# First block of a fused attention and two-layer kernel: attention rounds that overlap, low halves made on VectorE instead of GpSimd, and w_in stored in 4 KB rows

## The chip, the cores and the metric

One core of a Trainium2 chip runs the whole program. The metric is the device time of one execution in microseconds (us). A profiled execution has a span of its own, from the first to the last instruction that the trace shows, and a time beside it.

## The reference

The input is q, k and v of 4 batches, 8 heads, 576 positions and 64 dimensions, so 2304 tokens of width 512. Three layers follow each other.

```
scores = q @ k.T / 8, kept where 0 <= i - j < 64     # sliding window
x  = softmax(scores) @ v                              # 2304 x 512
h  = x @ w_in                                         # 512 -> 2048
x2 = softplus(h) @ w_out                              # max(h,0) + log1p(exp(-|h|)), 2048 -> 512
e  = argmax(x2 @ w_gate + bias[modality]),  p = softmax at e
out = p * (relu(x2 @ w1[e]) @ w2[e])                  # 8 experts, 512 -> 1024 -> 512
```

w_in and w_out come as 64-bit floats. Products are wanted to float32 accuracy.

## The kernel before

TensorE multiplies in a rounded float32 (F32R), so each operand is split: a high half (the value cast to F32R) and a low half (the value minus its high half, made by the helper `diff`, L88). A product is the sum of three matmuls: high by high, high by low, low by high.

The tokens are cut into 6 blocks of 384 (`b`), the 2048 hidden columns into 16 slices of 128 (`f`). A block's attention is 6 chunks of 64 tokens (`c`, so chunks 0 to 5 belong to block 0). One chunk goes through `a_scores` (scores and mask on TensorE, row maximum on VectorE, exponentials on ScalarE), `a_norm` (VectorE: reciprocal of the sum; the multiplication on VectorE for block 0 and on GpSimd for the others), `a_probs` (transposes on TensorE, copy on ScalarE) and `a_av` (times v on TensorE; `xh` by ScalarE, `xl` by VectorE). Tiles: `pss` scores, `s` probabilities, `pp` transposes, `pav` the product with v.

`mm1(b, f)` makes the hidden slice `ph` from 12 matmuls, which read the block's whole `xh` and `xl`, so it can't start before the last chunk's halves are there. It then makes softplus and its halves `gh` and `gl`. `mm2(b, f)` adds the slice to the three accumulators `px` with 9 matmuls, two slices later (LAG = 2). One such step is called a round here.

While block 0 runs, the weights are made as well: `w_load(f)` fetches 1 MB of slice f (half of it w_in, half w_out) into `raw`, and `w_decode(f)` turns the 64-bit floats into float32 by integer steps: ScalarE takes the absolute value (L222), VectorE clamps, shifts, and merges (L225 to L228), ScalarE casts the high half (L229), GpSimd makes the low half (L88 with tile `W`). The tile `wt` between L222 and L227 exists once. Slices 0 to 2 are decoded in two halves (w_in, then w_out). All weights stay on the chip, so blocks 1 to 5 have no decode.

Names for lines: L245 VectorE sets the sign bit, so that -|h| goes into the exponential; L246 and L247 are the exponential and logarithm on ScalarE, L248 adds max(h, 0) on VectorE, L251 casts `gh`. A scheduler orders each engine's instructions when the kernel is built; on the chip each engine then runs its list in order. `HOLD` makes it wait: the decodes of slices 1 and 2 come after the probabilities of chunks 4 and 5.

Of the kernel before, what the change touches and what calls it, by code (L numbers as in the profile page):

```python
# [19 lines left out]
P = 128  # L20
# [14 lines left out]
def attention_moe_moe_kernel(ctx, tc, q, k, v, w_in, w_out, modality, w_gate, mod_bias, w1, w2, out):  # L35
# [3 lines left out]
    HD = 64  # L39
    H = D // HD  # L40
    N = B * S
    F = w_in.shape[1]
    E, _, F2 = w1.shape
    KD = D // P
    NF = F // P
# [41 lines left out]
    def diff(eng, out_, a, hi):  # L87
        eng.tensor_tensor(out_, a, hi.bitcast(F32), ALU.subtract)  # L88

    at = {}  # L90
    marks = {}
    xblk = {}


# [22 lines left out]
    def a_scores(c, tags=None, s=None):  # L117
        w = at[c]
        win, n, qT, kT = w["win"], w["n"], w["q"], w["k"]
        if tags is None:  # L120
            both = ps.tile([P, 2, 4, P], F32, name="pss", tag="pS")
            parts = [both[:, :, 0:2, 0:n]]
            bank = [both[:, z, 0:2, 0:n] for z in range(2)]
        else:
            bank = [ps.tile([P, 2, P], F32, name=f"pss{z}", tag=tags[0], bufs=tags[1])[:, :, 0:n] for z in range(2)]
            parts = [x[:, None] for x in bank]
        for i in range(2):
            heads = [(2 * i + e, z) for e in range(2) for z in range(2)]
            outs = [bank[z][half(j, z) * C:(half(j, z) + 1) * C, i, :] for j, z in heads]
            for (j, z), o in zip(heads, outs):  # L130
                r = slice(z * C, (z + 1) * C)
                nc.tensor.matmul(o, qT[r, j, :], kT[r, :, j, :], start=True, stop=c >= BUSY)
            if c < BUSY:
                for (j, z), o in zip(heads, outs):
                    r = slice(z * C, (z + 1) * C)
                    nc.tensor.matmul(o, identb[r, r], mask[r, win], start=False, stop=True)
        s = sb.tile([P, 2, 2, P], F32, name="s") if s is None else s
        if c >= BUSY:
            nc.vector.tensor_tensor(s[:, :, :, 0:n], parts[0], mask[:, None, None, win].to_broadcast((P, 2, 2, n)), ALU.add)
            parts = [s[:, :, :, 0:n]]  # L140
            bank = [s[:, z, :, 0:n] for z in range(2)]
        mx = sb.tile([P, 2, 2], F32, name="mx")
        for i, x in enumerate(parts):
            nc.vector.tensor_reduce(out=mx[:, i:i + x.shape[1]], in_=x, axis=AX.X, op=ALU.max)
        nc.vector.tensor_scalar(mx, mx, -SCALE, None, ALU.mult)
        sm = sb.tile([P, NPR], F32, name="sm")
        for z in range(2):
            for i in range(2):
                marks['e', c] = nc.scalar.activation(s[:, z, i, 0:n], bank[z][:, i, :], AF.Exp, bias=mx[:, z, i:i + 1], scale=SCALE, accum_out=sm[:, 2 * z + i:2 * z + i + 1])
        w.update(s=s.rearrange("p z i k -> p (z i) k"), sm=sm)  # L150

    def a_norm(c):
        s, sm, n = at[c]["s"], at[c].pop("sm"), at[c]["n"]
        nc.vector.tensor_scalar(sm, sm, 1e-9, None, ALU.add)
        nc.vector.reciprocal(sm, sm)  # L155
        marks['n', c] = (nc.vector if c < CPB else nc.gpsimd).tensor_tensor(s[:, :, 0:n], s[:, :, 0:n], sm[:, :, None].to_broadcast((P, NPR, n)), ALU.mult)  # L156

    def a_probs(c, tag="pA", bufs=1, pT=None):
        s, n = at[c].pop("s"), at[c]["n"]
        pp = ps.tile([P, NPR, P], F32, name="pp", tag=tag, bufs=bufs)  # L160
        for j in range(NPR):
            nc.tensor.transpose(pp[0:n, j, :], s[:, j, 0:n], ident)
        pT = sb.tile([P, NPR, P], F32, name="pT", bufs=1) if pT is None else pT
        marks['p', c] = nc.scalar.copy(pT[0:n], pp[0:n])
        at[c]["pT"] = pT

    def a_av(c, tag="pA"):
        pT, n, vr = at[c].pop("pT"), at[c]["n"], at[c]["vr"]
        if c % CPB == 0:
            xblk[c // CPB] = (sb.tile([P, KD, TB], F32R, name="xh"), sb.tile([P, KD, TB], F32R, name="xl"))  # L170
        xh, xl = xblk[c // CPB]
        col = slice((c % CPB) * C, (c % CPB + 1) * C)
        po = ps.tile([P, NPR, C], F32, name="pav", tag=tag)
        for j in range(NPR):
            for z in range(2):
                r = slice(z * C, (z + 1) * C)
                nc.tensor.matmul(po[r, j, :], vr[0:n, j * P + z * C:j * P + (z + 1) * C], pT[0:n, 2 * z + j // 2, half(j, z) * C:(half(j, z) + 1) * C], start=True, stop=True)
        marks['v', c] = nc.scalar.copy(xh[:, :, col], po)
        diff(nc.vector, xl[:, :, col], po, xh[:, :, col])

    def attn_slots(b):
# [13 lines left out]

    W = {}
    raws = {}
    HOLD = {1: ('p', 4), 2: ('p', 5)}

    def wait_for(later, earlier, reason):  # L200
        tc.add_manual_dep(later.ins, earlier.ins.name, mybir.DependencyInfo(mybir.DependencyClass.Sync, mybir.DependencyReason.DATA), reason=reason)
# [1 line left out]
    def w_load(f, half=None):  # L203
# [1 line left out]
            raws[f] = wp.tile([P, 2, 512, 2], I32, name="raw", tag="W")  # L205
        raw = raws[f]
        if half != 1:
            nc.sync.dma_start(
                raw[:, 0].rearrange("p (k f) w -> p k (f w)", k=KD),
                w_in.bitcast(I32).rearrange("(k p) (f w) -> p k f w", p=P, w=2)[:, :, f * P:(f + 1) * P, :].rearrange("p k f w -> p k (f w)"))  # L210
        if half != 0:
            nc.sync.dma_start(raw[:, 1].rearrange("p f w -> p (f w)"), w_out.bitcast(I32)[f * P:(f + 1) * P, :])

    def w_decode(f):
# [20 lines left out]
    def mm1(b, f):  # L235
# [18 lines left out]

    px = {}
# [619 lines left out]
```

## Time and profile before

| what | us |
|---|---|
| median of 3 runs (lowest, highest) | 803.86 (803.25, 804.68) |
| the profiled execution: time | 805.67 |
| the profiled execution: span | 803.8 |
| mean granted TensorE clock in it | 0.968 |
| busy in the span: TensorE matmul / VectorE / ScalarE / GpSimd | 744.1 / 464.0 / 348.4 / 311.6 |

The time of an execution is about 2 us longer than its span, and the profiled one was some 2 us above the median of the others. The shares are averages over the attention of block 0, the rounds of block 0 with their decodes, five blocks without decodes, and the routed experts behind them.

### The profile page before, as it was taken

The page shows a single profiled execution, that of the slowest core. Times are in us where ns is not written, and L with a number is a line of the kernel's source. Part 1 is how long each engine was busy: PE and PEld are TensorE (multiplying, and loading weights), DVE is VectorE, ACT ScalarE, POOL GpSimd, SP SyncE. Part 2 cuts the span into 40 slices and gives each one's busy share as a digit, 9 for nine tenths or more (in the row PEclk, how much of TensorE's full clock was granted, in tenths as well). Part 3 has the DMA queues.
Part 4 walks back from the last instruction along what each step waited for, and adds up shares of the span by engine and source line. Part 5 has one row for each costly group of instructions (what it writes and reads, how often), then busy time and mean ns, then how long its engine had stood idle before and what let it go on. Part 6 is the DMA issues. An engine that isn't in the chain of part 4 may idle for free. (4 is left out here: it accounts for less than half of the span.)

```text
span 803.8 us, 12803 instructions
## 1 busy us (share of the span) xinstructions
PE 744.1 (93%) x4527; PEld 623.2 (78%) x4527; DVE 464.0 (58%) x1030; ACT 348.4 (43%) x827; POOL 311.6 (39%) x309
## 2 busy tenths in 40 slices
PE   5568878999999999999999999989989999999995
PEld 4457667888878888888878888878868888888884
DVE  4899999397459533964298428863533223223242
ACT  4655556554454554545355543544222122222243
POOL 3247565332423421342233322472273443443301
PEclk9669999999999999999999999999999999999998
DMA  8846531510232111311040103315021111111100
GB/s 316 250 153 206 167 107 46 178 53 21 60 100 66 35 46 44 108 27 48 14 144 1 28 14 112 138 32 231 15 73 37 55 48 36 52 52 45 39 28 17
DMA packets 48411, 65.17 MB, mean 81 GB/s; under 512 B 12797, under 2 KB 33661, under 8 KB 48200
## 3 DMA queue, kind: packets, MB, share of 16 engines
q1 hardware_dynamic: 43800, 54.45, 21.0%
q0 software_dynamic: 4528, 9.74, 3.7%
q8 instruction: 37, 0.61, 0.3%
q14 instruction: 46, 0.38, 0.2%
HBM read 54.37 MB, written 10.06 MB: 80 GB/s over the span
## 5 line engine op out<-in xcount | busy, mean ns | idle before, releaser
L88 POOL TENSOR_TENSOR gl<-a,gh 128x384 fp32r<-128x384 f32 x96 | 112.4, 1172 | 203.7 <-ACT gh L251 104.1
L240 PE MATMUL ph<-xh,W 128*128 128x384 f32 x384 | 136.8, 359 | 15.2 <-DVE a L248 14.9
L241 PE MATMUL ph<-xl,W 128*128 128x384 f32 x384 | 134.5, 350 | 0.8 <-DVE xl L88 0.8
L242 PE MATMUL ph<-xh,W 128*128 128x384 f32 x384 | 133.6, 348 | 0.0
L264 PE MATMUL px<-W,gh 128*128 128x512 f32 x288 | 115.9, 402 | 0.0
L265 PE MATMUL px<-W,gh 128*128 128x512 f32 x288 | 114.0, 396 | 0.0
L266 PE MATMUL px<-W,gl 128*128 128x512 f32 x288 | 105.9, 400 | 1.2 <-POOL gl L88 1.1
L246 ACT ACTIVATE a<-a 128x384 f32<-128x384 f32 x96 | 50.3, 524 | 116.4 <-DVE a L245 116.3
L240 PEld LDWEIGHTS ph<-xh,W 128*128 128x128 f32 x384 | 75.0, 196 | 24.6 <-DVE a L248 18.9
L245 DVE TENSOR_SCALAR a<-ph 128x384 int32<-128x384 int32 x96 | 52.9, 551 | 54.1 <-PE ph L242 52.2
L626 POOL DMA_INDIRECT gx<-x2s,pieces x76 | 73.7, 970 | 23.6 <-issue 13.9
L248 DVE SCALAR_TENSOR_TENSOR a<-ph,a 128x384 f32<-128x384 f32 x96 | 53.0, 552 | 45.5 <-ACT a L247 45.3
L241 PEld LDWEIGHTS ph<-xl,W 128*128 128x128 f32 x384 | 75.0, 195 | 4.7 <-DVE xl L88 1.6
L242 PEld LDWEIGHTS ph<-xh,W 128*128 128x128 f32 x384 | 74.8, 195 | 0.2
L251 ACT CAST gh<-a 128x384 fp32r<-128x384 f32 x96 | 49.1, 512 | 48.9 <-DVE a L248 45.0
L266 PEld LDWEIGHTS px<-W,gl 128*128 128x128 f32 x288 | 53.1, 188 | 14.1 <-POOL gl L88 2.5
L655 PE MATMUL p<-w,x2h 128*128 128x512 f32 x152 | 62.5, 411 | 1.2 <-ACT x2h L641 1.2
L88 POOL TENSOR_TENSOR W<-raw,W 128x1024 fp32r<-128x1024 f32 (+1 forms) x19 | 44.3, 2332 | 48.0 <-ACT W L229 48.0
L156 POOL TENSOR_TENSOR s<-s,sm 128x512 f32<-128x512 f32 (+1 forms) x30 | 34.5, 1150 | 72.6 <-DVE sm L155 51.1
L264 PEld LDWEIGHTS px<-W,gh 128*128 128x128 f32 x288 | 54.1, 188 | 10.9 <-issue 1.7
L693 POOL DMA_INDIRECT out_dram<-o,mg x19 | 19.3, 1017 | 107.8 <-ACT o L692 102.3
L265 PEld LDWEIGHTS px<-W,gh 128*128 128x128 f32 x288 | 54.3, 188 | 8.6
(192 smaller groups left out, 1420.5 us busy)
## 6 DMA issues: line engine op xcount, KB each, us to landing
raw<-in_moe_w_in_dram SPq DMA_DIRECT2D x16, 512.0 KB
raw<-in_moe_w_out_dram SPq DMA_DIRECT2D x16, 512.0 KB
r<-in_moe_w_dram SPq DMA_DIRECT2D x8, 1024.0 KB
qk<-in_k_dram SPq DMA_DIRECT2D x27, 256.0 KB
vr<-in_v_dram SPq DMA_DIRECT2D x27, 256.0 KB
qk<-in_q_dram SPq DMA_DIRECT2D x30, 128.0 KB
x2s<-xr SPq DMA_DIRECT2D x15, 256.0 KB
early<-in_v_dram SPq DMA_DIRECT2D x5, 256.0 KB
```

The source lines that it names most:

```text
L88: eng.tensor_tensor(out_, a, hi.bitcast(F32), ALU.subtract)
L240: nc.tensor.matmul(ph, W[f][:, 0, 0, sl], xh[:, c, :], start=c == 0, stop=False)
L241: nc.tensor.matmul(ph, W[f][:, 0, 0, sl], xl[:, c, :], start=False, stop=False)
L242: nc.tensor.matmul(ph, W[f][:, 0, 1, sl], xh[:, c, :], start=False, stop=c == KD - 1)
L245: nc.vector.tensor_scalar(a.bitcast(I32), ph.bitcast(I32), SIGN, None, ALU.bitwise_or)
L246: nc.scalar.activation(a, a, AF.Exp)
L248: nc.vector.scalar_tensor_tensor(a, ph, 0.0, a, ALU.max, ALU.add)
L264: nc.tensor.matmul(px[b][t], gh[:, sl], W[f][:, 1, 0, :], start=f == 0, stop=False)
L265: nc.tensor.matmul(px[b][t], gh[:, sl], W[f][:, 1, 1, :], start=False, stop=False)
L266: step["mm2"] = nc.tensor.matmul(px[b][t], gl[:, sl], W[f][:, 1, 0, :], start=False, stop=f == NF - 1)
L626: g = nc.gpsimd.indirect_dma_start(out=xr[:, c].rearrange("p c d -> p (c d)"), out_offset=None, in_=x2s[0:rows, :].rearrange("n (r f) -> ( ...
L655: first = nc.tensor.matmul(p, ah(c), bh(c), start=c == 0, stop=False)
```

## The change

Four things change, all in the part of the program that runs until block 0 is done.

1. Attention of block 0: the loop over rounds starts the scores of chunk i before it finishes chunk i-1, puts the product with v one round later (i-3), and the two `HOLD` waits go. The decodes of slices 0 and 1 are written into rounds 1 and 6 instead of 3 and 7. The order of the first loads changes with it.
2. Low halves: `W`'s are made by VectorE in every decode, `gl` by VectorE in block 0 and by GpSimd after it.
3. In block 0 ScalarE takes the absolute value of `ph` and a scale of -1 in the exponential, instead of VectorE's sign step. For block 1's attention (chunks 6 to 11) ScalarE multiplies by the reciprocals, four activations to a chunk, instead of one GpSimd operation.
4. w_in lies in memory by slice, 128 rows of 4 KB to a slice, instead of four runs of 1 KB to a row.

```diff
     def a_norm(c):
...
-        marks['n', c] = (nc.vector if c < CPB else nc.gpsimd).tensor_tensor(s[:, :, 0:n], s[:, :, 0:n], sm[:, :, None].to_broadcast((P, NPR, n)), ALU.mult)
+        if CPB <= c < BUSY:
+            for i in range(NPR):
+                nc.scalar.activation(s[:, i, 0:n], s[:, i, 0:n], AF.Copy, scale=sm[:, i:i + 1])
+        else:
+            (nc.vector if c < CPB else nc.gpsimd).tensor_tensor(s[:, :, 0:n], s[:, :, 0:n], sm[:, :, None].to_broadcast((P, NPR, n)), ALU.mult)
...
-    HOLD = {1: ('p', 4), 2: ('p', 5)}
...
-            nc.sync.dma_start(
-                raw[:, 0].rearrange("p (k f) w -> p k (f w)", k=KD),
-                w_in.bitcast(I32).rearrange("(k p) (f w) -> p k f w", p=P, w=2)[:, :, f * P:(f + 1) * P, :].rearrange("p k f w -> p k (f w)"))
+            nc.sync.dma_start(raw[:, 0].rearrange("p f w -> p (f w)"), w_in.bitcast(I32)[f])
...
-            d_ = nc.scalar.activation(tf, hf, AF.Abs)
-            if f in HOLD:
-                wait_for(d_, marks[HOLD[f]], 'attention first')
+            nc.scalar.activation(tf, hf, AF.Abs)
...
-            diff(nc.gpsimd, w[:, h, 1, :], hf, w[:, h, 0, :])
+            diff(nc.vector, w[:, h, 1, :], hf, w[:, h, 0, :])
...
-        nc.vector.tensor_scalar(a.bitcast(I32), ph.bitcast(I32), SIGN, None, ALU.bitwise_or)
-        nc.scalar.activation(a, a, AF.Exp)
+
+        if b == 0:
+            nc.scalar.activation(a, ph, AF.Abs)
+            nc.scalar.activation(a, a, AF.Exp, scale=-1.0)
+        else:
+            nc.vector.tensor_scalar(a.bitcast(I32), ph.bitcast(I32), SIGN, None, ALU.bitwise_or)
+            nc.scalar.activation(a, a, AF.Exp)
...
-        diff(nc.gpsimd, gl, a, gh)
+        diff(nc.gpsimd if b else nc.vector, gl, a, gh)
...
-    for part, c in [('qk', 0), ('qk', 1), ('v', 0), (0, 0), ('qk', 2), ('v', 1), ('v', 2), ('v', 3), ('v', 4), ('v', 5), (0, 1), (1, 0), (0, 2), (1, 1), (1, 2), ('qk', 6), ('v', 6), (0, 3), (1, 3)]:
+    for part, c in [('qk', 0), (0, 0), ('qk', 1), ('v', 0), (1, 0), ('qk', 2), ('v', 1), ('v', 2), ('v', 3), (0, 1), ('v', 4), ('v', 5), (1, 1), (0, 2), (1, 2), ('qk', 6), ('v', 6), (0, 3), (1, 3)]:
...
-    for i in range(CPB + 2):
+    for i in range(CPB + 3):
+        if i < CPB:
+            a_scores(i, ("px", TPB) if i % 2 else None, sb.tile([P, 2, 2, P], F32, name="s0", tag="xo", bufs=3))
+        if i in [1, 6]:
+            w_decode([1, 6].index(i))
         if 1 <= i <= CPB:
             a_norm(i - 1)
-        if i >= 2:
+        if i >= 3:
+            a_av(i - 3)
+        if 2 <= i < CPB + 2:
             a_probs(i - 2, "ph", 2, work if i % 2 else None)
-        if i >= 2:
-            a_av(i - 2)
-        if i < CPB:
-            a_scores(i, ("px", TPB) if i % 2 else None, sb.tile([P, 2, 2, P], F32, name="s0", tag="xo", bufs=3))
-        if i in [3, 7]:
-            w_decode([3, 7].index(i))
```

The engines' lists move at three places. The first is VectorE's list before, one round in the second half of block 0: one decode (L225 to L228 on `wt` and `raw`), the sign step and the sum of softplus (`a`).

```order
L225 TENSOR_SCALAR wt<-wt 128x1024
L248 SCALAR_TENSOR_TENSOR a<-ph,a 128x384
L226 TENSOR_SCALAR wt<-wt 128x1024
L227 SCALAR_TENSOR_TENSOR raw<-raw,wt 128x1024
L245 TENSOR_SCALAR a<-ph 128x384
L228 SCALAR_TENSOR_TENSOR raw<-raw 128x1024
```

In the changed kernel VectorE's list of such a round reads as follows (line numbers are shifted by a few: the decode is L223 to L226, L251 is the sum, and L88 makes the low halves of `W` and `gl`).

```order
L88 TENSOR_TENSOR W_1056<-raw,W_1056 128x2x512
L225 SCALAR_TENSOR_TENSOR raw<-raw,wt 128x1024
L251 SCALAR_TENSOR_TENSOR a<-ph,a 128x384
L88 TENSOR_TENSOR gl<-a,gh 128x384
L226 SCALAR_TENSOR_TENSOR raw<-raw 128x1024
L223 TENSOR_SCALAR wt<-wt 128x1024
L143 TENSOR_REDUCE mx<-pss 128x4
L88 TENSOR_TENSOR gl<-a,gh 128x384
L224 TENSOR_SCALAR wt<-wt 128x1024
```

The sign step is gone, one operation of 128x1024 and one of 128x384 have come. The second place is VectorE's list before, where the attention of block 0 ends: the two `xl` rows are chunks 4 and 5, and around them stand the last steps of slices 1 and 2 (128x512) and the first step of slice 3.

```order
L226 TENSOR_SCALAR wt<-wt 128x512
L88 TENSOR_TENSOR xl<-pav,xh 128x4x64
L228 SCALAR_TENSOR_TENSOR raw<-raw 128x512
L227 SCALAR_TENSOR_TENSOR raw<-raw,wt 128x512
L154 TENSOR_SCALAR sm<-sm 128x4
L228 SCALAR_TENSOR_TENSOR raw<-raw 128x512
L155 RECIPROCAL sm<-sm 128x4
L225 TENSOR_SCALAR wt<-wt 128x1024
L88 TENSOR_TENSOR xl<-pav,xh 128x4x64
```

In the changed list the `xl` of chunk 5, the last row here, stands behind all of slices 3 and 4 (`W_627` is slice 4) and behind the first two steps of slice 5.

```order
L88 TENSOR_TENSOR xl<-pav,xh 128x4x64
L226 SCALAR_TENSOR_TENSOR raw<-raw 128x1024
L143 TENSOR_REDUCE mx<-pss 128x4
L223 TENSOR_SCALAR wt<-wt 128x1024
L316 TENSOR_SCALAR scr_639<-mraw 128x18
L317 TENSOR_SCALAR scr_639<-mraw 128x18
L144 TENSOR_SCALAR mx<-mx 128x4
L88 TENSOR_TENSOR W_627<-raw,W_627 128x2x512
L224 TENSOR_SCALAR wt<-wt 128x1024
L320 TENSOR_TENSOR btok<-scr_639,bias_119 128x144
L320 TENSOR_TENSOR scr_639<-scr_639,bias_119 128x144
L88 TENSOR_TENSOR xl<-pav,xh 128x4x64
```

Counted from the top of the list, 3 slices were decoded ahead of that row before, and 5 are now. The third place is ScalarE's list in a round of block 0, before.

```order
L222 ACTIVATE wt<-raw 128x1024
L251 CAST gh<-a 128x384
L229 CAST W_1109<-raw 128x2x512
L246 ACTIVATE a<-a 128x384
L247 ACTIVATE a<-a 128x384
```

In the changed kernel the absolute value of `ph` (L245) and, every second round or so, the four products of `a_norm` (L157) stand between them; L246 is the exponential, L250 the logarithm and L254 the cast of `gh`.

```order
L222 ACTIVATE wt<-raw 128x1024
L245 ACTIVATE a<-ph 128x384
L246 ACTIVATE a<-a 128x384
L227 CAST W_1056<-raw 128x2x512
L157 ACTIVATE s<-s,sm 128x128 x4
L250 ACTIVATE a<-a 128x384
L254 CAST gh<-a 128x384
```

ScalarE's list of a round grows by one activation of 128x384 and, in half of the rounds, by four of 128x128.

## Rows read from the trace of the kernel before

**Rows 1.** Windows: start:end, length, busy us (x instructions) of each engine, granted clock, DMA.

```profile
8.96:28.35 19.39, 15.50 (x188) 11.67 (x188) 13.70 (x40) 13.05 (x58) 3.36 (x2) 0.93 1.00 346
...
42.90:138.10 95.20, 74.94 (x441) 61.91 (x442) 94.72 (x103) 53.31 (x104) 59.71 (x32) 0.89 0.43 143
138.10:155.20 17.10, 17.10 (x105) 13.50 (x105) 5.91 (x12) 7.97 (x17) 7.43 (x6) 1.00 0.35 113
155.20:750.00 594.80, 582.61 (x3440) 492.31 (x3439) 316.33 (x824) 243.06 (x594) 221.58 (x226) 0.99 0.20 62
```

**Rows 2.** Waits between 40 and 140 us: total, times, longest.

```profile
ACT wt L222 <- DVE raw L227: 31.9, 10, 4.1
...
PE ph L240 <- DVE a L248: 11.6, 8, 2.0
```

**Rows 3.** Timeline of VectorE: start, duration, line; one merge with GpSimd busy, the last decode.

```profile
110.50 3.35 DVE L227 SCALAR_TENSOR_TENSOR raw<-raw,wt 128x1024 int32<-128x1024 int32 x1
...
135.77 1.23 DVE L228 SCALAR_TENSOR_TENSOR raw<-raw 128x1024 int32<-128x1024 int32 x1
```

**Rows 4.** Timeline of GpSimd beside that merge.

```profile
109.88 2.89 POOL L88 TENSOR_TENSOR W<-raw,W 128x1024 fp32r<-128x1024 f32 x1
```

**Rows 5.** Timeline of VectorE where GpSimd does nothing.

```profile
70.95 0.68 DVE L225 TENSOR_SCALAR wt<-wt 128x1024 f32<-128x1024 f32 x1
71.67 0.69 DVE L226 TENSOR_SCALAR wt<-wt 128x1024 int32<-128x1024 int32 x1
72.39 1.23 DVE L227 SCALAR_TENSOR_TENSOR raw<-raw,wt 128x1024 int32<-128x1024 int32 x1
...
84.08 0.54 DVE L245 TENSOR_SCALAR a<-ph 128x384 int32<-128x384 int32 x1
84.55 1.21 DVE L228 SCALAR_TENSOR_TENSOR raw<-raw 128x1024 int32<-128x1024 int32 x1
85.68 0.68 DVE L225 TENSOR_SCALAR wt<-wt 128x1024 f32<-128x1024 f32 x1
```

**Rows 6.** Groups of VectorE by shape, 28.3 to 138.2 us: count, busy us, mean ns.

```profile
L227 DVE SCALAR_TENSOR_TENSOR raw<-raw,wt 128x1024 int32<-128x1024 int32 x13 | 32.3, 2483 | 0.3
L228 DVE SCALAR_TENSOR_TENSOR raw<-raw 128x1024 int32<-128x1024 int32 x13 | 18.1, 1392 | 0.0
L226 DVE TENSOR_SCALAR wt<-wt 128x1024 int32<-128x1024 int32 x13 | 15.6, 1201 | 0.1
L225 DVE TENSOR_SCALAR wt<-wt 128x1024 f32<-128x1024 f32 x13 | 11.2, 864 | 0.4 <-ACT wt L222 0.4
```

**Rows 7.** Timeline of VectorE at the end of block 0's attention.

```profile
31.64 0.69 DVE L227 SCALAR_TENSOR_TENSOR raw<-raw,wt 128x512 int32<-128x512 int32 x1
...
34.30 1.68 DVE L228 SCALAR_TENSOR_TENSOR raw<-raw 128x512 int32<-128x512 int32 x1
35.90 1.26 DVE L225 TENSOR_SCALAR wt<-wt 128x512 f32<-128x512 f32 x1
...
43.82 0.41 DVE L88 TENSOR_TENSOR xl<-pav,xh 128x256 fp32r<-128x256 f32 x1
```

**Rows 8.** Timeline of TensorE: first matmuls of block 0; one round of block 1.

```profile
42.96 1.01 PE L240 MATMUL ph<-xh,W 128*128 128x384 f32 x2 [0.25 <-ACT xh L178]
...
46.05 0.53 PE L240 MATMUL ph<-xh,W 128*128 128x384 f32 x1
...
160.85 0.66 PE L162 MATMUL pp<-ident,s 128*128 128x128 f32 x4
...
177.10 0.44 PE L240 MATMUL ph<-xh,W 128*128 128x384 f32 x1
...
181.39 0.34 PE L240 MATMUL ph<-xh,W 128*128 128x384 f32 x1
```

**Rows 9.** Groups of ScalarE by shape, 42.9 to 155.2 us.

```profile
L246 ACT ACTIVATE a<-a 128x384 f32<-128x384 f32 x16 | 8.4, 524 | 3.7 <-DVE a L245 3.7
...
L149 ACT ACTIVATE s<-pss,mx 128x128 f32<-128x128 f32 x12 | 4.3, 367 | 1.7 <-DVE mx L145 1.7
```

More of the change, by code (lines that the diff above doesn't have):

```diff
@@ L41, in attention_moe_moe_kernel @@
     N = B * S
-    F = w_in.shape[1]
+    F = w_out.shape[0]
     E, _, F2 = w1.shape
@@ L90, in attention_moe_moe_kernel @@
     at = {}
-    marks = {}
     xblk = {}
@@ L148, in a_scores @@
             for i in range(2):
-                marks['e', c] = nc.scalar.activation(s[:, z, i, 0:n], bank[z][:, i, :], AF.Exp, bias=mx[:, z, i:i + 1], scale=SCALE, accum_out=sm[:, 2 * z + i:2 * z + i + 1])
+                nc.scalar.activation(s[:, z, i, 0:n], bank[z][:, i, :], AF.Exp, bias=mx[:, z, i:i + 1], scale=SCALE, accum_out=sm[:, 2 * z + i:2 * z + i + 1])
         w.update(s=s.rearrange("p z i k -> p (z i) k"), sm=sm)
@@ L163, in a_probs @@
         pT = sb.tile([P, NPR, P], F32, name="pT", bufs=1) if pT is None else pT
-        marks['p', c] = nc.scalar.copy(pT[0:n], pp[0:n])
+        nc.scalar.copy(pT[0:n], pp[0:n])
         at[c]["pT"] = pT
@@ L177, in a_av @@
                 nc.tensor.matmul(po[r, j, :], vr[0:n, j * P + z * C:j * P + (z + 1) * C], pT[0:n, 2 * z + j // 2, half(j, z) * C:(half(j, z) + 1) * C], start=True, stop=True)
-        marks['v', c] = nc.scalar.copy(xh[:, :, col], po)
+        nc.scalar.copy(xh[:, :, col], po)
         diff(nc.vector, xl[:, :, col], po, xh[:, :, col])
@@ L861 @@
             a = a.reshape(b, h // 2, 2, s // 64, 64, d).transpose(0, 3, 2, 5, 1, 4).reshape(b, s // 64, 2 * d, h // 2 * 64)
+        if name == "moe_w_in":
+            a = a.reshape(4, 128, -1, 128).transpose(2, 1, 0, 3).reshape(-1, 128, 512)
         if name == "v":
```

## The prediction

> **What bounds the kernel now.** I read the windows first. From 155.20 to 750 us TensorE is busy 582.61 of 594.80 us at a clock of 0.99: there it is the bound, and the change edits nothing there. From 42.90 to 138.10 us, the rounds of block 0, VectorE is busy 94.72 of 95.20 us and TensorE 74.94; from 138.10 to 155.20 TensorE is full again (17.10 of 17.10) [rows 1]. So what can be won lies ahead of 155.2 us, where block 1's first `mm1` starts. The waits say the same: TensorE's `mm1` waits 11.6 us for VectorE's sum L248, and ScalarE's next decode waits 31.9 us for VectorE's merge L227 [rows 2].
>
> The question is then why VectorE is full. The merge L227 takes 3.35 us at 110.50 [rows 3]; GpSimd makes a low half of `W` from 109.88 for 2.89 us, to 112.77 [rows 4], and the merge ends 1.08 us after that, about its own length. Where GpSimd is idle the same merge takes 1.23 us, L228 1.21, L226 0.69, L225 0.68 [rows 5]. So VectorE's "busy" holds waiting for GpSimd.
>
> **What the change removes on VectorE.** From 28.3 to 138.2 us there are 13 full decodes [rows 6]. Mean less the free duration, times 13: L227 (2.483 - 1.23) x 13 = 16.3 us, L226 (1.201 - 0.69) x 13 = 6.6, L228 (1.392 - 1.21) x 13 = 2.4, L225 (0.864 - 0.68) x 13 = 2.4; sum 27.7. The half decodes lose some too: L228 at 34.30 takes 1.68 where the like merge L227 takes 0.69, and L225 at 35.90 takes 1.26 for 512 columns, more than the 0.68 of 1024 [rows 5, 7]; I put these and the small steps that stand behind a GpSimd operation at 4 us, so **-31.7 us**. In the changed order GpSimd has two fills in the rounds of block 0 and no tensor operation, so nearly all of this should go. Bounds: 27.7 is what full decodes alone show; nothing, if the wait isn't GpSimd's.
>
> The Trainium skill ("SBUF — State Buffer", the section on SBUF's two separate sides) has it that VectorE and GpSimd share a port pair as an exclusive lock, held for a whole instruction, and that VectorE meets it only in its two-port modes or with two SBUF inputs. By that all 59.71 us of GpSimd's work could block VectorE, where the rows of the four steps show 27.7 us lost: this trace bears out the lock, but not that every GpSimd operation costs its full length, because VectorE passes steps that read PSUM meanwhile. By the page's upper end VectorE would be far ahead and TensorE alone would set the end, at 137 (below).
>
> **What it adds there.** A low half of `W` reads two SBUF tensors like L228; the pitch from L228 to the next step is 85.68 - 84.55 = 1.13 us [rows 5]. 13 full ones 14.7, six half ones at 0.60 3.6: **+18.3 us**. The 16 sign steps (0.54 each [rows 5]) go and 16 operations for `gl` of the same 384 columns come: 0. Net on VectorE -31.7 + 18.3 = -13.4 us.
>
> **Attention first or decodes first.** The changed list has two more slices ahead of the last `xl` of block 0, which all of `mm1` waits for. Counted from the list: of slice 3 three more steps, slice 4 all four, slice 5 two (2.9 + 3.5 + 1.2 us at pitches 0.60 and 1.13), low halves of slices 0 to 4 (6 x 0.60 + 2 x 1.13 = 5.9), small steps 1.2: 14.7 us. Against it, 2.3 us of GpSimd's blocking before 43.82 (1.0 and 0.85 in two rows [rows 7], an estimate of 0.45 for the rest), and part of VectorE's idle time in the first attention rounds, 19.39 - 13.70 = 5.7 us [rows 1], since scores now run one round ahead and decodes fill gaps; I take 3 of the 5.7 and keep 0 and 5.7 as ends. So the first `mm1` moves from 42.96 [rows 8] to 42.96 + 14.7 - 2.3 - 3 = **52.4 us** (49.7 to 55.4), and then finds five slices ready.
>
> **From there to block 1.** TensorE needs, per round, 181.39 - 177.10 = 4.29 us at full clock [rows 8]: 16 rounds 68.6. The attention of chunks 6 to 11, three groups to a chunk of about the 0.66 us of the four transposes [rows 8], with masks, less the scores done earlier and plus some of block 2's: 12.7 (an estimate; 11 to 14). The first 20 or so matmuls run at half clock, 0.53 against 0.34 us [rows 8], as they do before: 3. So TensorE alone: 52.4 + 84.3 = 136.7. VectorE alone: its last decode step ends at 135.77 + 1.23 = 137.0 [rows 3]; less 13.4, less 3 of idle, plus 5 for waits for ScalarE that were hidden before (0 to 10): 125.6. Behind the last low half TensorE still has, by the lists, `mm1` of the last slice or two, four `mm2` and a chunk's remainder: 13.5 us, to 139.1. Two engines end within 3 us of each other, in a fixed order, so each will sometimes wait for the other; I add 4 us (0 to 10; no row prices this) and get **143 us** for block 1's start, against 155.2: **-12 us**.
>
> **ScalarE.** It is busy 53.31 of 95.20 us in the rounds [rows 1]. It gains 16 absolute values at 0.52 us like L246, and 24 products at about the 0.37 us of L149's 128 columns [rows 9]: 8.4 + 8.9 = 17.3 us; it also loses its waits. Over the 90 us that remain it would be some 80% busy: hidden, but no longer with much cover. If VectorE or TensorE needs such a result at once, an absolute value adds 0.52 us to the path of softplus in place of VectorE's 0.54, so the path stays.
>
> **The rows of w_in and the loads.** The queues are full at the start (DMA share 1.00 at 346 GB/s [rows 1]) and no wait for a weight stands in the rounds [rows 2]. Faster rows can only help before the first chunks; I take 0 (bounds 0 and -1, about one load of 0.5 MB at 346 GB/s, 1.5 us, done in half the time). The load of the first w_out now goes ahead of q and k of chunks 2 to 5: another 1.5 us at the same rate, inside the bounds of the start above. The Trainium skill ("DMA: Bandwidth & Descriptors", Specifications) gives 512 B as the least transfer for full rate; by that rows of 1 KB were already as good and the term is 0 as taken.
>
> **Sum.** Span 803.8 - 12 = 791.8; the profiled execution's own time is 805.67, so 793.7 for it. The runs' median, 803.86, is 1.8 below the profiled one; 803.86 - 12 = **792**.
>
> **The rivals.**
> *The attention comes too late* (the other side). TensorE can't begin before the last `xl`; the rest takes it 84.3 us plus the 4 of mutual waiting. If the first `mm1` starts at 67 us, block 1 starts at 155.3 and nothing is won; at 72 us the kernel takes 5 us more, 809. It needs 15 to 20 us of new idle time on VectorE in the attention rounds, say one wait of 1 us ahead of each of the decode steps now set between them. For it: VectorE idled 5.7 of 19.4 us there [rows 1]. Against: it idled with less to do. 9 in 100.
> *ScalarE becomes the bound.* With the list in fixed order and 80% busy, a wait of 0.5 us in each of 16 rounds gives 8 us back: 800. For: the 17.3 us it gains; against: it waited 31.9 us for VectorE before [rows 2], which now answers sooner. 15 in 100.
> *The change doesn't free VectorE.* If the long merges come from something other than GpSimd, 18.3 us are added to a full engine: 822. Against: the end of each long merge follows GpSimd's [rows 3, 4]. 4 in 100.
>
> **How the numbers follow.** The forecast, -7 to -17 us (no extra waits, the upper rows of every bound, against all of them), has 68 in 100; 4 are left for no change from mixed small losses. A measurement of this kernel tells about 0.2%, 1.6 us, from no change. Faster by more: 68 + 15 = 83. Within: 4 and 2 of the late attention, 6. Slower: 7 and 4, 11. The forecast's own range is 787 to 797; to hold 8 in 10 it takes in ScalarE's case, so 785 to 801.
>
> **What would show it.** In the changed trace: merges of 128x1024 at 1.2 us throughout; GpSimd without tensor work until block 1; the first `mm1` near 52 us, VectorE's last low half near 126, block 1's `mm1` near 143, and the stretch from there to the end as long as before, 803.8 - 155.2 = 648.6 us. Wrong it would be with the first `mm1` past 60 us, merges that stay above 2 us, or a longer stretch behind block 0, which I hold for unchanged because its instructions are.

## The result, and the profile after

| | before | changed |
|---|---|---|
| median of 4 runs (lowest, highest), us | 803.57 (803.25, 804.68) | 780.74 (779.96, 781.97) |
| the profiled execution: time / span, us | 805.67 / 803.8 | 781.15 / 779.1 |
| mean granted clock in it | 0.968 | 0.978 |

The ratio is 0.9714, with a 95% interval of 0.9702 to 0.9725: 22.8 us faster. The forecast was 792 us, with 785 to 801 as the range, so the sign was right and the size was not: 11 us more came than I gave, and the time lies below the range.

The windows of the changed kernel come first, with the columns of [rows 1].

```profile
9.00:30.00 21.00, 14.52 (x184) 10.99 (x184) 20.34 (x55) 15.01 (x51) 0.00 (x0) 0.97 1.00 351
30.00:43.00 13.00, 6.77 (x80) 5.24 (x80) 12.95 (x24) 11.00 (x31) 0.00 (x0) 0.50 0.73 248
43.00:60.00 17.00, 12.90 (x70) 11.49 (x70) 16.78 (x29) 13.71 (x35) 0.00 (x0) 0.72 0.59 205
60.00:80.00 20.00, 19.85 (x175) 15.74 (x174) 19.04 (x34) 18.88 (x51) 0.00 (x0) 1.00 0.71 234
80.00:100.00 20.00, 20.00 (x133) 16.04 (x132) 18.31 (x30) 17.93 (x40) 0.00 (x0) 1.00 0.51 170
100.00:120.00 20.00, 20.00 (x127) 16.36 (x126) 17.77 (x26) 13.74 (x30) 1.04 (x1) 1.00 0.23 71
120.00:140.00 20.00, 20.00 (x122) 16.41 (x121) 8.30 (x18) 10.51 (x26) 1.04 (x1) 1.00 0.41 162
```

The reader is to see two things. GpSimd's column is zero from 9 to 100 us. And from 60 us on TensorE is busy 79.85 of 80 us at full clock, where it had 74.94 of 95.20 at 0.89 in the rounds before [rows 1]: the bound has moved from VectorE to TensorE. VectorE's own groups, 20 to 130 us (line, shapes, count, busy us, mean ns, idle time before), answer to [rows 6]:

```profile
L88 DVE TENSOR_TENSOR W<-raw,W 128x1024 fp32r<-128x1024 f32 x13 | 15.9, 1221 | 3.8 <-ACT W L227 3.7
L225 DVE SCALAR_TENSOR_TENSOR raw<-raw,wt 128x1024 int32<-128x1024 int32 x13 | 15.8, 1218 | 0.0
L226 DVE SCALAR_TENSOR_TENSOR raw<-raw 128x1024 int32<-128x1024 int32 x13 | 15.8, 1215 | 0.0
L224 DVE TENSOR_SCALAR wt<-wt 128x1024 int32<-128x1024 int32 x13 | 8.9, 687 | 0.1
L223 DVE TENSOR_SCALAR wt<-wt 128x1024 f32<-128x1024 f32 x13 | 8.9, 681 | 0.3 <-ACT wt L222 0.3
```

The four decode steps now have the durations that [rows 5] showed where GpSimd is idle. Their 13 full decodes took 32.3 + 18.1 + 15.6 + 11.2 = 77.2 us [rows 6] and take 15.8 + 15.8 + 8.9 + 8.9 = 49.4 us: 27.8 us less, where 27.7 was forecast. GpSimd's timeline shows why:

```profile
6.44 0.37 POOL L313 MEMSET scr<- 128x152 int32 x1
115.39 1.04 POOL L159 TENSOR_TENSOR s<-s,sm 128x512 f32<-128x512 f32 x1 [108.58 <-DVE sm L154]
```

It does nothing between 6.8 and 115.4 us. The waits from 40 to 140 us answer to [rows 2]; ScalarE's wait for the merge fell from 31.9 to 4.8 us, and VectorE now waits for ScalarE's cast of `W`, five times:

```profile
ACT wt L222 <- DVE raw L225: 4.8, 5, 2.2
...
DVE W L88 <- ACT W L227: 3.7, 5, 2.3
```

What did not come as forecast is seen on TensorE's timeline (block 0's first `mm1`; its first matmul that reads `xl`; block 1's first `mm1`):

```profile
43.76 1.01 PE L238 MATMUL ph<-xh,W 128*128 128x384 f32 x2 [1.39 <-ACT xh L181]
...
46.59 0.69 PE L239 MATMUL ph<-xl,W 128*128 128x384 f32 x1
...
136.66 0.52 PE L238 MATMUL ph<-xh,W 128*128 128x384 f32 x2
```

Block 0's first `mm1` stands at 43.76, not at 52.4; block 1's at 136.66, not at 143. The matmuls at 43.76 read `xh` alone: it is not all of `mm1` that waits for the last `xl`, as the description of the kernel has it. The first matmul that reads `xl` comes at 46.59 us, and before the change at 44.28. On VectorE's timeline the first decode step, the last `xl` of block 0 and the last low half of `W` are:

```profile
6.62 0.47 DVE L223 TENSOR_SCALAR wt<-wt 128x512 f32<-128x512 f32 x1 [0.21 <-ACT wt L222]
...
45.80 0.42 DVE L88 TENSOR_TENSOR xl<-pav,xh 128x256 fp32r<-128x256 f32 x1
...
121.24 1.23 DVE L88 TENSOR_TENSOR W<-raw,W 128x1024 fp32r<-128x1024 f32 x1 [2.33 <-ACT W L227]
```

The first matmul of each block, and the end of the last `mm2`, in us:

| | block 0 | 1 | 2 | 3 | 4 | 5 | last `mm2` ends | span |
|---|---|---|---|---|---|---|---|---|
| before | 42.96 | 155.24 | 239.04 | 320.10 | 403.67 | 485.29 | 557.55 | 803.8 |
| changed | 43.76 | 136.66 | 218.13 | 298.42 | 382.11 | 461.81 | 533.65 | 779.1 |

So 18.6 us of the 24.7 by which the spans differ come before block 1, and 6.1 behind it. In the experiments I read block 2's first `mm1`, because every kernel here has started the same 1471 TensorE instructions by then, and again 3085 at block 5's; in between, and at block 1's (881 before, 913 changed), they differ by some chunks' scores.

### The profile page after: what moved, and what is told of

Same layout as the page of the kernel before. It is cut to its first block, busy times and chain, and to the rows that moved or that the text cites. A ratio compares the mean times of both kernels' runs of the same rounds, so it can differ in the third digit from the quotient of the medians.

```text
span 779.1 us, 12784 instructions
## 1 busy us (share of the span) xinstructions
PE 735.8 (94%) x4527; PEld 617.7 (79%) x4527; DVE 448.2 (58%) x1049; ACT 361.6 (46%) x867; POOL 236.4 (30%) x268
## 5 line engine op out<-in xcount | busy, mean ns | idle before, releaser
L88 POOL TENSOR_TENSOR gl<-a,gh 128x384 fp32r<-128x384 f32 x80 | 89.3, 1117 | 176.6 <-ACT gh L254 112.2
L238 PE MATMUL ph<-xh,W 128*128 128x384 f32 x384 | 133.5, 350 | 7.6 <-DVE a L251 6.1
L239 PE MATMUL ph<-xl,W 128*128 128x384 f32 x384 | 131.3, 342 | 0.8 <-DVE xl L88 0.8
L240 PE MATMUL ph<-xh,W 128*128 128x384 f32 x384 | 131.0, 341 | 0.0
L249 ACT ACTIVATE a<-a 128x384 f32<-128x384 f32 x80 | 42.0, 525 | 104.2 <-DVE a L248 104.1
L159 POOL TENSOR_TENSOR s<-s,sm 128x512 f32<-128x512 f32 (+1 forms) x24 | 26.0, 1082 | 199.3 <-DVE sm L154 173.9
L238 PEld LDWEIGHTS ph<-xh,W 128*128 128x128 f32 x384 | 72.7, 190 | 15.4 <-DVE a L251 8.1
L239 PEld LDWEIGHTS ph<-xl,W 128*128 128x128 f32 x384 | 72.8, 190 | 4.2 <-DVE xl L88 1.5
L248 DVE TENSOR_SCALAR a<-ph 128x384 int32<-128x384 int32 x80 | 44.1, 551 | 51.6 <-PE ph L240 48.8
L251 DVE SCALAR_TENSOR_TENSOR a<-ph,a 128x384 f32<-128x384 f32 x96 | 53.0, 552 | 35.7 <-ACT a L250 35.6
L240 PEld LDWEIGHTS ph<-xh,W 128*128 128x128 f32 x384 | 73.0, 190 | 0.2
L254 ACT CAST gh<-a 128x384 fp32r<-128x384 f32 x96 | 49.0, 512 | 47.3 <-DVE a L251 45.6
L658 PE MATMUL p<-w,x2h 128*128 128x512 f32 x152 | 62.3, 410 | 1.2 <-ACT x2h L644 1.2
L661 PE MATMUL p<-w,x2h 128*128 128x512 f32 x152 | 60.4, 397 | 0.0
L662 PE MATMUL p<-w,x2l 128*128 128x512 f32 x152 | 60.3, 398 | 0.0
```

Source lines behind the costliest of these rows:

```text
L238: nc.tensor.matmul(ph, W[f][:, 0, 0, sl], xh[:, c, :], start=c == 0, stop=False)
L239: nc.tensor.matmul(ph, W[f][:, 0, 0, sl], xl[:, c, :], start=False, stop=False)
L658: first = nc.tensor.matmul(p, ah(c), bh(c), start=c == 0, stop=False)
L661: nc.tensor.matmul(p, ah(c), bl(c), start=False, stop=False)
L662: nc.tensor.matmul(p, al(c), bh(c), start=False, stop=c == n - 1)
```

## The experiments

Each kernel is compared with the kernel before on its own chip. On the chips of e1 to e4 and e9 to e12 that kernel takes 811.8 and 811.6 us, on that of e5 to e8 804.4. e4 has the changed kernel's order of work, so on its chip it can stand for that kernel. The scheduler builds the lists anew for every edit, so instructions that an edit doesn't touch can stand elsewhere too; only e4 and e8 have the lists of the changed kernel and of the kernel before.

**e1: the low halves of `W` back on GpSimd.**

```diff
-            diff(nc.vector, w[:, h, 1, :], hf, w[:, h, 0, :])
+            diff(nc.gpsimd, w[:, h, 1, :], hf, w[:, h, 0, :])
```

> The changed kernel with the low halves of W made by GpSimd again; all else stays changed. If VectorE's blocking by GpSimd was the price (theory), VectorE sheds 18 us of its own work, but its merges of 128x1024 go back from 1.22 us to 2 us and more, and the kernel is 8 to 20 us slower than the changed one (789 to 801 us). If the low halves don't matter and the new attention order alone brought the 23 us (rival), it stays within 4 us of 781.

Measured: 811.44 against 811.79 us, ratio 0.9992 (0.9978 to 1.0005); the whole gain is gone. Groups of VectorE, then GpSimd, from 20 to 150 us:

```profile
L225 DVE SCALAR_TENSOR_TENSOR raw<-raw,wt 128x1024 int32<-128x1024 int32 x13 | 30.4, 2340 | 0.4
...
L224 DVE TENSOR_SCALAR wt<-wt 128x1024 int32<-128x1024 int32 x13 | 13.7, 1055 | 0.1
...
L88 POOL TENSOR_TENSOR W<-raw,W 128x1024 fp32r<-128x1024 f32 x13 | 34.4, 2648 | 58.2 <-ACT W L227 54.6 <-DMA raw<-in_moe_w_in_dram 3.7
```

The merge is back at 2.34 us, twice the changed kernel's 1.22. VectorE has some 20 us less to do than in the changed kernel (it makes no low half of `W`), and the kernel is 23.4 us slower than e4. Of these, 19.6 us are there at block 2's first `mm1` (237.75 against 218.19).

**e2: the ScalarE moves undone** (sign step on VectorE, products of chunks 6 to 11 on GpSimd).

```diff
-        if CPB <= c < BUSY:
+        if c < 0:
...
-        if b == 0:
+        if b < 0:
```

> The changed kernel with the sign step on VectorE and the products of chunks 6 to 11 on GpSimd again. Theory: TensorE is full from 60 us on and VectorE some 90% busy, so 16 x 0.47 = 7.5 us more on VectorE and six operations on GpSimd that block it cost 2 to 7 us (783 to 788). Rival: ScalarE, 94% busy between 60 and 80 us, was the tighter one; then it is 1 to 4 us faster (777 to 780).

Measured: 797.92 us, 0.9831 (0.9804 to 0.9858), 9.9 us over e4 and so more than expected. In the trace 4.7 us of it are there at block 2's first `mm1` (222.80 against 218.13). Nearly all of the rest comes in blocks 2 and 3, which take 168.61 us against the changed kernel's 163.98, part of it under a lowered clock (below). No edited instruction stands there, so this part is the order of the later lists and the clock.

**e3: loop, holds and load order of attention as before.**

```diff
+    HOLD = {1: ('p', 4), 2: ('p', 5)}
...
-    for i in range(CPB + 3):
+    for i in range(CPB + 2):
...
```

> The changed kernel with the attention loop, the holds and the order of the first loads as before. Theory: the 8.6 us by which my forecast had the first mm1 too late came from here (VectorE's first decode step at 6.6 instead of 9.0 us, its idle time of 5.7 us filled), so these come back: 4 to 10 us slower than the changed kernel (785 to 791), with VectorE idle 4 to 6 us before 30 us. Rival: only VectorE's total work counts and the order is worth nothing: within 1.6 us of 781.

Measured: 791.77 us, 0.9750 (0.9731 to 0.9769), 3.7 us over e4, a little less than expected. Its first `mm1` stands at 43.80, as in the changed kernel, yet block 2's at 220.33, 2.2 us later. The window shows where VectorE lost the time; the changed kernel's VectorE is busy 20.34 of 21 us there.

```profile
9.00:28.35 19.35, 16.47 (x187) 12.60 (x187) 13.99 (x41) 12.70 (x56) 0.00 (x0) 1.00 0.98 348
```

**e4: w_in in runs of 1 KB again.**

```diff
...
-            nc.sync.dma_start(raw[:, 0].rearrange("p f w -> p (f w)"), w_in.bitcast(I32)[f])
+            nc.sync.dma_start(
+                raw[:, 0].rearrange("p (k f) w -> p k (f w)", k=KD),
+                w_in.bitcast(I32).rearrange("(k p) (f w) -> p k f w", p=P, w=2)[:, :, f * P:(f + 1) * P, :].rearrange("p k f w -> p k (f w)"))
...
```

> The changed kernel with w_in in runs of 1 KB again. Theory: the longer rows help only until the first chunks are in: 0 to 2 us slower (781 to 783). Rival: the 2.3 us of earlier start and more of the gain behind it come from the rows, through fuller queues in the first 40 us: 3 to 6 us slower (784 to 787).

Measured: 788.04 us, 0.9706 (0.9693 to 0.9719); the rows give nothing. The block starts repeat the changed kernel's to within 0.07 us (136.70, 218.19, 298.48). The first decode step starts at 6.97, close to 6.62; so the earlier start comes from the order of the loads. e3, with the old order of loads and the new rows, starts at 8.44; e12, with the new order and the old rows, at 6.52. In all five traces ScalarE's step that releases it waits for this very load: it starts at 8.26 us before and at 5.92 in the changed kernel. The Trainium skill ("DMA: Bandwidth & Descriptors", Specifications) has 512 B as the least transfer at full rate, by which 1 KB runs lose nothing: this run agrees.

**e5: the kernel before, with the low halves of `W` on VectorE** (e1's edit the other way round).

> The kernel before with one edit: VectorE makes the low halves of W. Theory (GpSimd's blocking is the price, the parts need each other): the merges fall to 1.2 to 1.4 us, VectorE saves 20 to 27 us of blocking and adds 18, GpSimd's gl still blocks now and then: 3 to 9 us faster than the kernel before. Rival: this part is the whole change, 17 us or more.

Measured: 794.83 against 804.39 us, 0.9880 (0.9865 to 0.9895): 9.6 us, just above what was expected. The merge L227 falls from 2483 [rows 6] to 1405 ns, with `gl` and the products still on GpSimd.

**e6: the kernel before, with fills by GpSimd in place of its low halves of `W`.** VectorE's instructions are those of before; some stand in another order, most of these behind 120 us. The kernel leaves the low halves of `W` out: zeros stand in their place.

```diff
-            diff(nc.gpsimd, w[:, h, 1, :], hf, w[:, h, 0, :])
+            nc.gpsimd.memset(w[:, h, 1, :].bitcast(F32), 0.0)
```

> The kernel before, in which GpSimd writes zeros for the low halves of W instead of subtracting (the low-half products then add nothing). VectorE's work stays as it was. Theory: what holds VectorE is a GpSimd operation that reads; the merge L227 falls from 2.48 to at most 1.4 us on average and the kernel gains 12 to 20 us. Rival 1: any GpSimd operation holds it for its length; with writes of about 1 us the merge takes 1.7 to 2.1 us and the gain is 5 to 10 us. Rival 2: the long merges don't come from GpSimd; no gain.

Measured: 783.49 us, 0.9738 (0.9714 to 0.9763). 20.9 us come with another operation on GpSimd, while VectorE's instructions are the same. Its 13 full decodes take 61.7 us in place of 77.2 [rows 6]. Groups from 20 to 150 us:

```profile
L228 DVE SCALAR_TENSOR_TENSOR raw<-raw 128x1024 int32<-128x1024 int32 x13 | 18.0, 1381 | 0.0
L227 DVE SCALAR_TENSOR_TENSOR raw<-raw,wt 128x1024 int32<-128x1024 int32 x13 | 16.9, 1300 | 0.3
L225 DVE TENSOR_SCALAR wt<-wt 128x1024 f32<-128x1024 f32 x13 | 14.3, 1104 | 0.4 <-ACT wt L222 0.4
L226 DVE TENSOR_SCALAR wt<-wt 128x1024 int32<-128x1024 int32 x13 | 12.5, 962 | 0.1
...
L230 POOL MEMSET W<- 128x1024 f32 x13 | 13.5, 1040 | 0.4 <-ACT W L229 0.4
```

The merge is nearly free of waiting (1300 ns against 1230 alone), but L225 got longer than before (1104 against 864 [rows 6]). One stretch of the timelines shows the fills holding it; VectorE's row first, then GpSimd's:

```profile
41.32 4.78 DVE L225 TENSOR_SCALAR wt<-wt 128x1024 f32<-128x1024 f32 x1 [0.44 <-ACT wt L222]
...
41.02 1.04 POOL L156 TENSOR_TENSOR s<-s,sm 128x512 f32<-128x512 f32 x1 [4.11 <-DVE sm L155]
42.00 0.95 POOL L230 MEMSET W<- 128x1024 f32 x1
42.89 0.61 POOL L309 MEMSET scr<- 128x608 int32 x1
43.44 0.95 POOL L230 MEMSET W<- 128x1024 f32 x1
44.33 0.37 POOL L310 MEMSET scr<- 128x152 int32 x1
44.55 1.01 POOL L230 MEMSET W<- 128x1024 f32 x1
```

A step of 0.68 us [rows 5] lasts 4.78, through the rest of a product (L156) and five fills that follow each other without a gap, and ends 0.5 us after the last. VectorE counts as busy all that time.

**e7: the changed kernel, with slice 3's decode held until `xh` of chunk 5.** It puts the attention first again.

```diff
...
+    HOLD = {3: ('v', 5)}
...
-            nc.scalar.activation(tf, hf, AF.Abs)
+            d_ = nc.scalar.activation(tf, hf, AF.Abs)
+            if f in HOLD:
+                wait_for(d_, marks[HOLD[f]], 'attention first')
```

> The changed kernel with slice 3's decode held until the high half of chunk 5 is made, so that three slices instead of five are decoded ahead of the last xl. Theory A (TensorE, full from 60 us on, sets block 0's end): the first mm1 comes 4 to 7 us earlier, and with it the end: 3 to 6 us faster than the changed kernel. Theory B (VectorE's whole work sets it): the first mm1 comes earlier, TensorE then waits for weights, and the time is within 1.6 us of the changed kernel's.

Measured: 785.87 us, 0.9773 (0.9758 to 0.9787), so (0.9773 - 0.9714) x 804.39 = 4.7 us slower than the changed kernel. Neither theory had that. The first `mm1` comes 1.7 us earlier (42.08), and block 2's 2.6 us later (220.73). Its windows:

```profile
28.35:43.00 14.65, 11.01 (x147) 8.69 (x144) 8.37 (x25) 12.42 (x48) 0.00 (x0) 0.50 0.50 185
...
43.00:60.00 17.00, 12.93 (x88) 11.40 (x87) 16.74 (x29) 12.51 (x26) 0.00 (x0) 0.78 0.54 180
...
100.00:120.00 20.00, 19.04 (x169) 15.45 (x169) 18.54 (x31) 16.43 (x42) 0.00 (x0) 1.00 0.60 194
120.00:140.00 20.00, 16.06 (x105) 13.19 (x104) 16.82 (x28) 13.47 (x35) 5.31 (x3) 1.00 0.48 161
```

VectorE is busy 8.37 of the 14.65 us in which it is held and loses 6.3. From 43 to 60 us TensorE is busy as long as in the changed kernel (12.93 and 12.90); the loss is paid 60 us later, from 100 to 140, where it is busy 35.10 of 40 us and in the changed kernel 40.00.

**e8: the kernel before once more**, one profile and one time.

> The kernel before once more, for a second trace of it. Of the 24.7 us between the two profiled spans 6.1 lie behind block 0. If that is in the order of the lists, blocks 1 to 5 take the same times as in the first trace (83.8, 81.1, 83.6, 81.6, 72.3 us); if it is chance, they shift by 1 us and more, and the clock dip at 330 us is gone.

Measured: 804.6 us, span 802.7. The lengths of its blocks 1, 2 and 4 are within 0.06 us of the first profile's; block 3 takes 82.28 us instead of 83.57.

**e9: `gl` of block 0 back on GpSimd.**

```diff
-        diff(nc.gpsimd if b else nc.vector, gl, a, gh)
+        diff(nc.gpsimd, gl, a, gh)
```

> The changed kernel with gl of block 0 made by GpSimd again. VectorE sheds 16 x 0.47 = 7.5 us, GpSimd reads again for 16 x 1.2 us or so. Theory (each GpSimd read costs VectorE about its own length where VectorE is full): it loses 8 to 15 us of blocking for 7.5 saved: 1 to 6 us slower than the changed kernel. Rival: VectorE passes steps that read PSUM meanwhile, and the saving wins: 1 to 4 us faster.

Measured: 789.38 against 811.64 us, 0.9724 (0.9710 to 0.9739): no difference from the changed kernel that the times show, where one side or the other was expected. The first groups of VectorE, 20 to 130 us:

```profile
L225 DVE SCALAR_TENSOR_TENSOR raw<-raw,wt 128x1024 int32<-128x1024 int32 x13 | 19.4, 1495 | 0.0
L88 DVE TENSOR_TENSOR W<-raw,W 128x1024 fp32r<-128x1024 f32 x13 | 17.4, 1342 | 0.9 <-ACT W L227 0.7
L226 DVE SCALAR_TENSOR_TENSOR raw<-raw 128x1024 int32<-128x1024 int32 x13 | 16.8, 1294 | 0.1
```

Against the changed kernel's 15.8, 15.9 and 15.8 us these lose 6.1 us to GpSimd's 16 operations, where VectorE spends 16 x 0.60 = 9.6 us if it makes them: the two prices are near each other.

**e10: the products of chunks 6 to 11 on VectorE** instead of ScalarE.

```diff
-        if CPB <= c < BUSY:
+        if c < 0:
...
-            (nc.vector if c < CPB else nc.gpsimd).tensor_tensor(...)
+            (nc.vector if c < BUSY else nc.gpsimd).tensor_tensor(...)
```

> The changed kernel with the products of chunks 6 to 11 on VectorE, one operation of 128x512 to a chunk, instead of four on ScalarE. VectorE gains 6 x 0.6 = 3.6 us, ScalarE sheds some 6.5 us. Theory (VectorE's whole work sets block 0's end): 2 to 5 us slower. Rival (VectorE's 6 us of idle time between 60 and 122 us, most of it for ScalarE's casts, are what is left to win): 1 to 4 us faster.

Measured: 791.33 us, 0.9742 (0.9716 to 0.9768); the interval overlaps the changed kernel's, the trace has block 2's first `mm1` 4.0 us later, at 222.13. The window is the one in which ScalarE is fullest in the changed kernel:

```profile
60.00:80.00 20.00, 17.25 (x130) 14.38 (x129) 19.98 (x33) 16.33 (x34) 0.00 (x0) 0.91 0.53 193
```

ScalarE gets 2.6 us of room, VectorE is full again, and TensorE falls from 19.85 to 17.25 us.

**e11: the kernel before, with both kinds of low halves on VectorE** (the edits of e5 and, the other way round, e9).

> The kernel before with the low halves of W, and gl of block 0, made by VectorE; sign step, products, attention and rows as before. GpSimd then reads in block 0 only for six products of 1.2 us. Theory: VectorE adds 18.3 + 7.5 us and sheds nearly all of the 32 us of blocking: 6 to 10 us faster than the kernel before, no more than the low halves of W alone brought (9.7 us), and the rest of the change's 23 us needs the sign step off VectorE and the new attention. Rival: with GpSimd quiet nearly all comes: 16 us or more.

Measured: 804.99 us, 0.9913 (0.9896 to 0.9930). That is less than e5's gain with one kind alone: here `gl` is added to a VectorE that still has the sign step. The clock may have a part in it, since from 100 to 120 us it is 0.72 here and 1.00 in e5.

**e12: the kernel before, with the new attention loop and load order and no holds.**

> The kernel before with the new attention loop, the new order of the first loads and no holds; low halves, sign step, products and rows as before. Theory: VectorE begins 2 us earlier and its 5.7 us of idle time before 28 us fill up, so it ends 4 to 8 us earlier: 4 to 8 us faster than before. Rival: decodes brought forward only bring GpSimd's blocking forward, into the attention: within 1.6 us of before, or slower.

Measured: 813.22 us, 1.0026 (1.0011 to 1.0040), 1.6 us slower. The groups from 8 to 53.3 us show a decode step and a very small operation, both held:

```profile
L226 DVE TENSOR_SCALAR wt<-wt 128x1024 int32<-128x1024 int32 x3 | 4.7, 1552 | 0.0
L145 DVE TENSOR_SCALAR mx<-mx 128x4 f32<-128x4 f32 x7 | 4.1, 589 | 0.0
```

L226 takes 0.69 us alone [rows 5], and 128x4 elements take 0.16 in the changed kernel. As in the changed kernel, more decodes stand ahead of the last `xl`, but here GpSimd's blocking comes forward with them: that `xl` ends at 53.32 us, 9.1 later than before.

## Why the prediction was right in its mechanism and wrong in its size

**What bounds, and why VectorE is full: right.** e6 leaves VectorE its instructions and gets 20.9 us; e1 keeps all other parts and loses the whole gain. So the long merges were waits for GpSimd, and no ordinary work. The rival by which the change would not free VectorE is out.

The Trainium skill ("SBUF — State Buffer", the section on two separate sides) lets VectorE's operations with two SBUF inputs meet the lock only against a GpSimd operation that reads SBUF, and those in a two-port mode against any. e6 agrees: fills, which read no tensor, leave the two-input merge at 1300 ns. They hold the one-input step for 4.78 us, which fits if it runs in such a mode; no run here shows the mode.

**Removed 31.7, added 18.3: right.** The 27.7 us of full decodes were 27.8. The half decodes lost 2.3 us (15.6 to 13.3) and the small steps some 3.7, where 4 was put for both. The low halves of `W` take 15.9 us in 13 full and 4.0 us in six half operations, 19.9 in place of 18.3. The swap of the sign step for `gl`, put at 0, is 16 x 0.55 against 16 x 0.60.

**"So the first `mm1` moves from 42.96 to 52.4 us": the step that failed.** The term behind it is the last `xl`, put 9.4 us later; it ended 46.22 - 44.23 = 2.0 us later. The windows from the first decode step to the end of that `xl`, before and then changed, hold the account:

```profile
8.96:44.23 35.27, 23.52 (x290) 17.65 (x290) 29.03 (x73) 24.14 (x88) 10.14 (x7) 0.73 0.81 273
```

```profile
6.62:46.22 39.60, 24.55 (x310) 18.64 (x314) 38.86 (x93) 29.29 (x96) 0.19 (x1) 0.78 0.89 313
```

- VectorE's busy time grew by 38.86 - 29.03 = 9.8 us; 14.7 - 2.3 = 12.4 was forecast. The blocking that went was larger than 2.3 (four steps at 34.30, 35.90, 37.68 and 42.69 us alone lost 2.8, and small ones more) and the counted work somewhat smaller than 14.7.
- Its idle time fell from 6.2 to 0.7 us, by 5.5; I had taken 3 out of 0 to 5.7.
- The first decode step came 2.3 us earlier, by the new order of the loads (e4, e3, e12), which I had put as a possible cost of 1.5 us and not as a gain.

The three misses are 2.6 + 2.5 + 2.3 = 7.4 us, which is 9.4 - 2.0. The lower bound of 49.7 held the second alone. Taken on from there, this step and the next gave block 1's start 6.3 us earlier than the 143 forecast; with the 6.1 us behind block 0 (below), 792 - 6.3 - 6.1 = 779.6, beside the 780.74 measured.

**From there to block 1, 84.3 + 4 plus what VectorE's late end adds, 90.6 in all: nearly right, in part by luck.** It took 136.66 - 43.76 = 92.9 us. TensorE was busy 89.4 of them, where 84.3 was put; 112 score matmuls stand in this time, where 64 did before the change. The 2.4 us for VectorE's late end did not come and hid about half of this. TensorE was idle for 3.5 us, near the 4 of mutual waiting, but they are not spread over the rounds: 3.3 lie before 60 us, and next to nothing after. VectorE's last low half ended at 122.47, not 125.6, and 14.2 us ahead of block 1 (13.5 forecast).

e7 shows that an early start is worth nothing by itself: bought with idle time on VectorE, and with fewer slices ready, it lost 4.7 us. So it is VectorE's filled idle time that counts, and the early first `mm1` is only its sign.

**ScalarE at 0: right, and the rival of ScalarE as the bound is out.** It is busy 18.88 of 20 us at its fullest, and TensorE is full all the same. What I left out is how much hangs on these moves: undone together (e2) they cost 4.7 us by block 2's start, about half of the sign step's 16 x 0.55 = 8.7 us on VectorE. The other 5.2 of e2's 9.9 us come behind it.

**Attention too late: did not come,** since VectorE's idle time shrank where the rival needed 15 to 20 us more. The new order alone (e12) is slower, but there VectorE is busy 44.97 of 46.80 us from its first decode step to the last `xl`: with blocking, not idle.

**The rows of w_in at 0: right** (e4).

**"The stretch from there to the end as long as before": wrong by 6.1 us,** 648.6 to 642.4. The traces place nearly all of it. TensorE's time on the score tiles `pss` in block 1 is, before and then changed:

```profile
155.24:239.04 83.80, 6.22 (x128) 1.00 0.22 69
136.66:218.13 81.47, 4.47 (x96) 1.00 0.19 61
```

- At block 1's start the changed kernel has done 144 score matmuls on `qk` and the kernel before 112. These 32 are about 1.8 us (an estimate: eight take 0.45 us at full clock on TensorE's timeline) of the 2.3 by which block 1 is shorter.
- From block 2's to block 5's start, where both have done the same matmuls, the kernel before takes 246.25 us in its first profile, 244.91 in e8, and the changed kernel 243.68. The first 1.3 us are a lowered clock (below). The other 1.2 go with TensorE's idle time, 4.9 us in e8 and 3.5 in the changed kernel.
- Block 5 gives 0.4 us, and what lies behind the last `mm2` 0.8; why, stays open.

Blocks 3 and 4 can't be read one by one: block 4 takes 81.62 us in the lists of before and e6 and 79.69 to 79.71 in all the others, whichever the chip, but it holds 80 score matmuls in the one case and 48 in the other, and block 3 holds the difference. My reason, that the instructions behind block 0 are the same, passed over that their order is not.

**The parts together.** Undone one by one they cost 23.4, 9.9, 3.7 and 0 us, more than the gain; added one by one to the kernel before they give 9.6 us (e5), 6.7 with `gl` (e11) and a loss (e12). Part of these sums is the order of later lists (e2), so they are no exact prices. As e2 and e11 have it, the low halves on VectorE need room there, which the sign step's and the products' move makes; and the new attention order pays only once GpSimd is silent (e3, e12). No version that I ran beats the changed kernel.

## What to carry to other kernels

An engine that is "busy" for 99% of a stretch may be waiting inside its instructions: set the mean of one shape beside the same shape where the neighbour is idle, and if they differ, moving work onto the full engine can free it. When such a change also reorders the start, count three things apart for the engine that binds (when its first instruction starts, its work up to the next gate, and how much of its idle time is filled), and let the range take their bounds together. Undo the parts one at a time as well as adding them, since parts that need each other look small when added alone.

## What the runs showed of the hardware that was not expected

- Fills on GpSimd hold VectorE's one-input steps (4.78 us for a step of 0.68, through one product and five fills) while they leave the two-input merge nearly alone (1300 ns); the low half that reads two tensors held the merge (2.34 to 2.48 us) and one-input steps as well (L226 1201 ns for 690).
- The granted clock can fall for some us in one execution of a list and not in another (0.73 is a mean of 2.4 GHz and 1.2 GHz). The kernel before from 330 to 335 us, then the same in e8:

```profile
330.00:335.00 5.00, 5.00 (x21) 4.73 (x21) 4.77 (x16) 3.33 (x13) 3.93 (x4) 0.73 0.34 104
```

```profile
330.00:335.00 5.00, 5.00 (x27) 4.74 (x28) 5.00 (x15) 3.64 (x13) 3.89 (x3) 1.00 0.42 128
```

  In the 9.2 us before, from 320.0 to 329.2, TensorE is busy 7.59 us in the one and 7.60 in the other, at full clock in both; what made the difference, no run shows. In e2 the clock falls twice at block 2's start, each time after a stretch in which TensorE was idle for 2.5 and 2.7 us:

```profile
217.00:222.00 5.00, 2.55 (x56) 1.94 (x58) 4.55 (x13) 2.55 (x8) 1.08 (x1) 1.00 0.65 218
222.00:225.40 3.40, 3.20 (x22) 2.37 (x19) 3.26 (x11) 1.99 (x9) 0.00 (x0) 0.50 0.69 212
225.40:232.30 6.90, 4.18 (x35) 3.85 (x36) 6.76 (x19) 1.68 (x4) 1.36 (x1) 0.99 0.13 41
232.30:235.70 3.40, 3.40 (x34) 2.93 (x29) 3.40 (x10) 2.06 (x5) 1.19 (x2) 0.51 0.35 111
```

- Equal lists repeat to hundredths of a us on different chips: the changed kernel and e4 take 83.69 and 83.68 us for block 3, 79.70 and 79.72 for block 4. The difference of those two chips, 8.5 us in the spans, lies behind the last `mm2`, in the routed experts: 245.4 against 253.9 us.
